# Two layers of attention and token mixer on one core: the mixer's first product in two passes instead of three, a third conversion buffer for VectorE's exponentials, loads tied to VectorE, and another order at the end of a layer

## The chip, the core and the metric

The kernel runs on one core of a Trainium2 chip. The core has TensorE (matrix products, into PSUM), VectorE, ScalarE and GpSimd, and a fifth engine, SyncE, that here only issues DMAs. The profile calls them PE, DVE, ACT, POOL and SP; PEld is TensorE's loading of weights. Each engine runs its own queue of instructions in order and waits for the others by semaphores. The metric is the device time of one launch in microseconds (us), as a median of several runs.

## The reference

The input is one sequence of 2048 tokens of width 640. Two blocks alternate, A, B, A, B, with the same weights both times.

```
def _A_ref(x, wqkv, wo):            # 32 heads of 20
    qkv = (x @ wqkv) ... q, k, v
    scores = einsum("bhqd,bhkd->bhqk", q, k) * 20 ** -0.5
    p = softmax(scores);  o = einsum("bhqk,bhkd->bhqd", p, v)
    return o @ wo
def _B_ref(x, w1, b1, w2, b2):      # mixes tokens: 2048 -> 1536 -> 2048
    u = gelu(einsum("bsd,sf->bdf", layernorm(x), w1) + b1)
    return transpose(einsum("bdf,fs->bds", u, w2) + b2)
x = x + A(layernorm(x));  x = x + B(layernorm(x))      # twice
```

The heads are narrow (20), so the two attention products are small and the 2 x 32 x 2048 x 2048 exponentials are the large part of the work.

## The kernel before

**Attention.** The queries are cut into four blocks of 512 (qb 0 to 3), the 32 heads into 8 groups of 4 (g), the keys into 16 tiles of 128 (kt). A unit is (qb, g, kt): four scores of 128 keys by 512 queries, one for each head of the group, which are called chunks here. There are 2048 chunks in a layer. The last block is cut into two halves of 256 queries, so that its first half is done early. For each chunk TensorE makes the scores S (`s_matmul`, L638), something takes the exponential, and TensorE adds P times V to the PSUM tile acc (`emit_PV`, L1253). V has a column of ones, which gives the softmax's denominators.

**Who takes the exponential.** ScalarE takes most: `emit_exp` (L708) works through tiles of three and of two chunks in turn (S to P). VectorE takes the rest, in pairs of chunks, by an approximation in integer and float steps: `ew` (L537) moves a chunk out of PSUM as an integer, `ey` (L597) shifts its fraction, `ey*ey` (L567) squares it, `et` (L571) and `Pd` (L580) finish the pair. The step L597 can be done by GpSimd or by VectorE: `ve_shift` hands it to GpSimd where VectorE is about to run a step that the planner counts as free of the memory port that the two engines share, and with a dependency on that moment (`after_vector`). What GpSimd hasn't got by then is done by VectorE in `shifted`. `ve_admit` decides when a chunk goes to VectorE. It refuses while VectorE's planned backlog is over VE_BACKLOG us, or while too many pairs wait in `ve_procs`, and it picks the unit whose chunk it takes by the backlog plus VE_MARGIN. The integers of a pair lie in the pool `vew` (2 buffers).

**The planner.** All of this is written out by a Python program that keeps a clock for each engine with planned durations, and lays the instructions into the queues in the order in which its clocks say they can run. ScalarE gets its tiles one after the other. In the time that TensorE has between them, `slot_work` (L1309) puts PV products, pieces of other products ("fills", `add_fill` and `fill_step`), or, if there is nothing, products with a zero matrix (`zeros`, L697), which keep TensorE busy and change nothing. The order of the DMAs on SyncE is not written out but left to the framework's own scheduler, which goes by the dependencies that it knows.

**The rest of a layer as fills.** When a query block is done, `enqueue_outproj` (L1031) adds the output product, "O" (L1044), and its sums with x become the rows x1; `do_ln2` (L865) normalises a tile of 128 rows into h2. The mixer's first product, "M" (`enqueue_mm1_partial`, L974, matmuls L992), sums over tokens, so that it can be begun with the rows that are there. It goes through 12 tiles of 128 columns of w1 (ft), each in two halves of 320 columns. M_GROUPS says which row tiles make one pass: 0 to 3, 4 to 7, and 8 to 13 (TAIL = 2 tiles are left for the end). The first two passes write their sums to a DRAM buffer, `uacc`: the half rows leave PSUM through VectorE to `ustg` (L1005) and go out by a DMA of GpSimd's queue, the second pass's with addition in the DMA (L1013). The last pass fetches the sums back (`fetch_row`, L958, a SyncE DMA into the places of buffers that are done with) and adds to them in SBUF (L1000). Each pass loads its piece of w1 for a column tile just ahead (`mm1_prefetch`, L970, two buffers `w1st`). The normalised rows of the first two passes lie in four buffers `h2st`; the later ones in the big buffer `hh`, which by then is free. The O products of blocks 0 and 1 have a gate: none starts while M products are left (`m_left`).

**The end of a layer** (`end_tiles`, L882). When ScalarE has done its last tile, the last PV and the normalisation of the last head group remain (L745 to L769, `attnT`). Fills that are left over are put in first. Then ScalarE loads the table for gelu (L884), TensorE writes zeros to two PSUM tiles (L697 on S), ScalarE copies the last two row tiles of x1 into them (L891), TensorE adds the last part of O (L895, in the order odd, then tile), VectorE and GpSimd take the statistics, ScalarE copies the sums back (L906), and ScalarE and VectorE normalise one tile each (L920, L923). `mixer_head` (L1666 on) then adds the last two row tiles of M, takes gelu, and starts the second product. After layer 0 that second product is fill work beside the next layer's attention; after layer 1 it runs alone to the end. The weights `w1l` that `mixer_head` needs are loaded over K's rows during the last units (`load_w1l`, L164).

Of the kernel before, what the change touches and what calls it, by code (L numbers as in the profile page):

```python
# [12 lines left out]
BF16 = mybir.dt.bfloat16  # L13
# [5 lines left out]
ACT = mybir.ActivationFunctionType  # L19
ALU = mybir.AluOpType  # L20
# [3 lines left out]
D = 640  # L24
# [10 lines left out]
    A0_LAG=2,  # L35
    VE_BACKLOG=4.0,
    VE_MARGIN=2.0,
    VE_LEAST=4,
# [39 lines left out]
def kernel(  # L78
# [12 lines left out]
    nc = tc.nc  # L91
# [3 lines left out]
    NT = S // 128  # L95
    NKT = NT
    NQB = S // 512
    NF = F // 128
# [35 lines left out]
    TAIL = 2  # L134
    M_GROUPS = [list(range(4 * p, 4 * p + 4)) for p in range(NQB - 2)] + [list(range(4 * (NQB - 2), NT - TAIL))]
    IN_HH = 4 * (NQB - 2)
    assert NF % 2 == 0
    uacc = [dpool.tile([F, D], F32, name=f"uacc{i}") for i in range(2)]
# [3 lines left out]
    mhalf = consts.tile([128, 1], F32, name="mhalf")  # L142
# [10 lines left out]
    x1lp = ctx.enter_context(tc.tile_pool(name="x1lp", bufs=1))  # L153
    x1last = x1lp.tile([128, 4, D], F32, name="x1last")
    hhp = ctx.enter_context(tc.tile_pool(name="hhp", bufs=1))
    hh = hhp.tile([128, NDT * S], BF16, name="hh")
# [7 lines left out]
    def load_w1l():  # L164
        for sti in range(TAIL):
            nc.sync.dma_start(out=w1l_view[:, sti, :], in_=B_w1[(NT - TAIL + sti) * 128:(NT - TAIL + sti + 1) * 128, :])

# [49 lines left out]
    def attention(st, x_in_ap, x_mid, uacc_l, feed, feed_stack):  # L217
# [16 lines left out]
        def open_late():  # L234
            def pool(name, bufs):
                late[name] = p1.enter_context(tc.tile_pool(name=f"{name}{layer}", bufs=bufs, reuse_waits="tile"))
            pool("xsp", 3 if x_in_ap.dtype == F32 else 2)
            pool("h2sp", 4)
            pool("w1sp", 2)
            pool("ustg", 2)  # L240
            pool("atp", NG + 4)
            pool("vew", 2)
            pool("vet", 1)
            pool("vey", 2)
            pool("vep", 3)
# [254 lines left out]
        def ve_admit(t):  # L500
# [297 lines left out]
        at_live = [0]  # L798
        m_left = [0]
        fill_queue = []  # L800
# [64 lines left out]
        def do_ln2(tt, x1s, end):  # L865
            def dst():
                if tt >= IN_HH:
                    assert check_hT_dead()
                    h2_tiles[tt] = h2_view[:, tt, :]
                else:  # L870
                    h2_tiles[tt] = late["h2sp"].tile([128, D], BF16, name="h2st")[:]
                return h2_tiles[tt]

            def after(e):
                ln_open.remove(tt)
                p = next(i for i, grp in enumerate(M_GROUPS) if tt in grp)
                if all(i in h2_tiles for i in M_GROUPS[p]):
                    enqueue_mm1_partial(p, e + DVE_TO_PE)
            ln_open.append(tt)
            ln_proc(x1s[:], True, dst, 3, end + DVE_NEXT, after)  # L880

        def end_tiles(sums):  # L882
            assert check_hT_dead() and TAIL == 2
            nc.scalar.activation(out=warm_act[:, 0:1], in_=mhalf[:, 0:1], func=ACT.Gelu_apprx_tanh, scale=1.0)  # L884
            gp = NG // 2 - 1
# [4 lines left out]
            for t, x1 in zip(sums, x1_end):  # L890
                nc.scalar.copy(out=t[:, 0:D], in_=x1)  # L891
            for odd in range(2):
                for ttl, t in enumerate(sums):
                    for c0, c1 in Y_CUTS:
                        pe(nc.tensor.matmul(t[:, c0:c1], lhsT=attnT[:, 256 * odd + ttl * 128:256 * odd + (ttl + 1) * 128],  # L895
                                            rhs=wo_pad[:, 2 * gp + odd, c0:c1], start=False, stop=(odd == 1),
                                            skip_group_check=True))
# [46 lines left out]
        def fetch_row(ft):  # L944
            if ft >= NF or ft in fetched:
                return
            if ft == len(st.ua):
# [8 lines left out]
                else:  # L956
                    return
            nc.sync.dma_start(out=st.ua[ft], in_=uacc_l[ft * 128:(ft + 1) * 128, :])  # L958
            fetched[ft] = pem["t"] + 5.0
# [6 lines left out]
        def mm1_prefetch(p, ft):  # L966
            if ft < NF and (p, ft) not in w1_of:
                group = M_GROUPS[p]
                w1st = w1_of[(p, ft)] = late["w1sp"].tile([128, len(M_GROUPS[-1]), 128], BF16, name="w1st")
                nc.sync.dma_start(out=w1st[:, 0:len(group), :],  # L970
                                  in_=B_w1[group[0] * 128:(group[-1] + 1) * 128, ft * 128:(ft + 1) * 128].rearrange(
                                      "(a s) f -> s a f", s=128))

        def enqueue_mm1_partial(p, ready):  # L974
# [3 lines left out]
            direct = p == len(M_GROUPS) - 1  # L978
            m_left[0] += 2 * NF
            rows = {}  # L980
# [3 lines left out]
            for ft in range(NF):  # L984
                for ci, (c0, c1) in enumerate(((0, D // 2), (D // 2, D))):
                    w = c1 - c0
                    mms = []
                    for sti in range(n_in):
                        def mm(t, sti=sti, ft=ft, c0=c0, c1=c1, w=w, ci=ci):
                            if sti == 0 and ci == 0:  # L990
                                mm1_prefetch(p, ft + 1)
                            pe(nc.tensor.matmul(t[:, 0:w], lhsT=w1_of[(p, ft)][:, sti, :],  # L992
                                                rhs=rows_in[sti][:, c0:c1], start=(sti == 0), stop=(sti == n_in - 1)))
                            m_left[0] -= sti == n_in - 1
                        mms.append(mm)

                    def evac(t, end, eng, ft=ft, c0=c0, c1=c1, w=w):
# [23 lines left out]
                    add_fill("M", 1e3 + p, mms, evac, w, ready=ready + (4.0 if p < NQB - 2 else 0.0), allow=later,  # L1021
                             gate=(lambda ft=ft: row_here(ft)) if direct else None)
# [8 lines left out]
        def enqueue_outproj(qb, ready):  # L1031
# [3 lines left out]
            for ttl in range(4):  # L1035
                tt = qb * 4 + ttl
                for ci, (c0, c1) in enumerate(((0, D // 2), (D // 2, D))):
# [12 lines left out]
                    def evac(t, end, eng, tt=tt, c0=c0, c1=c1, w=w, ci=ci):  # L1050
# [6 lines left out]
                        if ci == 1:  # L1057
                            nc.sync.dma_start(out=x_mid[tt * 128:(tt + 1) * 128, :], in_=x1s[:])
                            do_ln2(tt, x1s, end)
                            del tt_state[tt]  # L1060
                    add_fill("O", prio, mms, evac, w, ready=ready, gate=(lambda: m_left[0] == 0) if qb < NQB - 2 else None,
                             allow=lambda me, tt=tt: not any(o <= tt - 2 for o in ln_open))

        def enqueue_outproj_last(half, pairs, ready):
# [3 lines left out]
            if half == 0:  # L1068
                mm1_prefetch(NQB - 2, 0)
                for ft in range(4):  # L1070
                    fetch_row(ft)
            for ttl in range(2):
                tt = tt0 + ttl
                for ci, (c0, c1) in enumerate(((0, D // 2), (D // 2, D))):
# [13 lines left out]
                    def evac(t, end, eng, tt=tt, c0=c0, c1=c1, w=w, ci=ci):  # L1088
# [707 lines left out]
```

## Time and profile before

| | |
|---|---|
| time, median of 3 runs | 1780.67 us (1779.75 to 1782.98) |
| the profiled execution | 1779.18 us, of which 1777.4 us are the span shown |
| ScalarE busy | 1686.8 us (95%) |
| TensorE busy, with the zero products | 1686.2 us (95%) |
| VectorE busy | 1537.8 us (87%) |
| GpSimd busy | 339.3 us (19%) |
| ScalarE tiles of 3 / 2 / 1 chunks | 724 / 724 / 2 |
| chunks on VectorE (L537) | 474, in 237 pairs |
| steps L597 on GpSimd / on VectorE | 392 / 82, of 617 / 419 ns |
| half rows to ustg (L1005) | 96 of 481 ns |
| DMAs uacc<-ustg | 48, of which 24 with addition (894 ns of GpSimd each) |
| granted TensorE clock | full in every stretch |

The span has five stretches: a start of some 17 us, layer 0's attention to 831.5 us, the mixer's head and the start of layer 1's attention (from 869.5 us), that attention to 1707 us, and the last mixer to the end. Busy time of one engine is the union of its instructions; the mean duration of one can be longer than its share, because neighbours overlap: ScalarE's 1450 exponentials of 1377 ns mean take 1639.3 us together. A busy TensorE says little here, since the zero products count as busy.

### The profile page before, as it was taken

What the parts mean: (1) busy time and instruction counts of PE and PEld (TensorE: products, weight loads), DVE (VectorE), ACT (ScalarE), POOL (GpSimd) and SP (SyncE); (2) the same over time, 40 slices, a digit from 0 to 9 for tenths busy, and PEclk for the clock granted to TensorE, in tenths of its full rate; (3) what the DMA queues carried; (4) which work ended last, traced back from release to release, by engine and by line L of the source; (5) the groups of instructions that cost most, each with busy time, mean ns of one, the idle gap of its engine ahead of it and who ended that gap; (6) DMA issues with size and microseconds to landing.
All of it is one profiled execution on the core that took longest, in us unless ns stands there. A gap on an engine that the chain in (4) does not pass through costs nothing.

```text
span 1777.4 us, 42841 instructions
## 1 busy us (share of the span) xinstructions
PE 1686.2 (95%) x17848; PEld 668.0 (38%) x17929; DVE 1537.8 (87%) x2429; ACT 1686.8 (95%) x1518; POOL 339.3 (19%) x519
## 2 busy tenths in 40 slices
PE   8999999999999999999999999999999999999999
PEld 3333333333333344444444433233333333444445
DVE  7479999999999999998543469999999999999972
ACT  8999999999999999998779999999999999999970
POOL 2111111122233221121000001222222331212100
PEclk9999999999999999999999999999999999999999
DMA  4200000011117110123322100001112460101235
GB/s 121 27 1 1 1 1 2 20 38 64 53 53 124 28 58 13 31 57 91 110 81 79 52 11 2 1 2 38 54 42 75 83 114 24 61 3 48 63 113 179
DMA packets 106851, 89.71 MB, mean 50 GB/s; under 512 B 51744, under 2 KB 88224, under 8 KB 106656
## 3 DMA queue, kind: packets, MB, share of 16 engines
q1 hardware_dynamic: 97664, 71.22, 13.7%
q0 software_dynamic: 8992, 15.75, 4.6%
q8 instruction: 140, 2.29, 0.6%
q14 instruction: 55, 0.45, 0.1%
HBM read 55.48 MB, written 31.46 MB: 49 GB/s over the span
## 4 chain that ended last, share of the span: by engine, by line
ACT 51%; issue 23%; PE 19%; DVE 3%; DMA 2%; SPq 0%; POOL 0%; another core or an unknown queue 0%; ACTq 0%; POOLq 0%; DVEq 0%
ACT P L708 51%; PE S L638 5%; PE acc L1253 2%; PE ya L1679 2%; PE misc L992 2%; PE acc L697 1%; PE misc L1104 1%; DMA uacc<-ustg 1%; PE um L1666 1%; DMA w1st<-in_B_w_dram 1%; DVE ew L537 1%; PE ya L1688 1%; DVE et L571 1%; PE yb L1679 1%; PE misc L1598 0%
## 5 line engine op out<-in xcount | busy, mean ns | idle before, releaser
L708 ACT ACTIVATE P<-S 128x1024 bf16<-128x1024 f32 (+1 forms) x1450 | 1639.3, 1377 | 15.5 <-PE S L638 15.2
L638 PE MATMUL S<-QTq,KT 32*128 32x512 bf16 (+1 forms) x4519 | 584.5, 337 | 70.1 <-ACT P L708 54.3
L597 POOL TENSOR_SCALAR ey<-ew 128x512 f16<-128x512 uint16 x392 | 242.0, 617 | 1039.5 <-DVE et L571 384.7
L638 PEld LDWEIGHTS <-KT 32*128 32x128 bf16 x5137 | 232.4, 91 | 531.8 <-issue 506.3
L1253 PE MATMUL acc<-P,Vaug 128*32 128x512 bf16 (+1 forms) x4502 | 366.0, 343 | 0.0
L537 DVE TENSOR_SCALAR ew<-Dt 128x512 int32<-128x512 f32 x474 | 323.6, 683 | 18.2 <-PE Dt L638 9.4
L697 PE MATMUL acc<-zr,zw 128*32 128x512 bf16 x4292 | 336.1, 384 | 1.3 <-POOL zr L151 1.2
L580 DVE SCALAR_TENSOR_TENSOR Pd<-ew,et 128x1024 int16<-128x1024 int16 x237 | 296.5, 1251 | 1.1
L571 DVE SCALAR_TENSOR_TENSOR et<-ey,ew 128x1024 f32<-128x1024 f16 x237 | 290.1, 1224 | 2.0
L638 PE MATMUL Dt<-QTq,KT 32*128 32x512 bf16 (+1 forms) x618 | 182.2, 332 | 0.0
L1253 PEld LDWEIGHTS <-Vaug 128*32 128x32 bf16 x5120 | 102.9, 94 | 177.7 <-issue 168.3
L567 DVE TENSOR_TENSOR ey<-ey 128x1024 f16<-128x1024 f16 x237 | 162.0, 684 | 5.0 <-POOL ey L597 0.9
L697 PEld LDWEIGHTS <-zw 128*32 128x32 bf16 x4504 | 113.6, 96 | 103.7 <-issue 60.7
L838 POOL TENSOR_TENSOR rstd<-veps,mhalf 128x1 f32<-128x1 f32 x60 | 50.5, 842 | 250.9 <-DVE veps L836 204.6
L1253 PE MATMUL acc<-Pd,Vaug 128*32 128x512 bf16 (+1 forms) x618 | 93.2, 334 | 0.0
L1104 PE MATMUL misc<-hh,wq_pad 128*128 128x512 bf16 x276 | 83.4, 383 | 2.2 <-issue 1.6
L992 PE MATMUL misc<-h2st,w1st 128*128 128x320 bf16 x384 | 74.6, 303 | 3.2 <-DMA w1st<-in_B_w_dram 2.5
L992 PEld LDWEIGHTS <-w1st 128*128 128x128 bf16 x672 | 52.3, 97 | 62.2 <-issue 45.7
L745 DVE STREAM_TRANSPOSE T<-acc 128x512 f32<-128x512 f32 (+1 forms) x81 | 56.3, 695 | 19.4 <-PE acc L1253 19.3
L1044 PE MATMUL misc<-wo_pad,attnT 128*128 128x320 bf16 x384 | 72.6, 302 | 0.2
L1104 PE MATMUL misc<-hh,wk_pad 128*128 128x512 bf16 x211 | 65.0, 383 | 2.5 <-issue 2.1
L357 DVE CAST KT<-misc 128x512 bf16<-128x512 f32 x48 | 32.9, 685 | 20.1 <-PE misc L1104 19.9
(144 smaller groups left out, 1161.0 us busy)
## 6 DMA issues: line engine op xcount, KB each, us to landing
uacc<-ustg POOLq DMA_DIRECT2D x48, 320.0 KB, 4.2
w2s<-in_B_w_dram SPq DMA_DIRECT2D x16, 768.0 KB
x1in<-xd SPq DMA_DIRECT2D x24, 320.0 KB
w1st<-in_B_w_dram SPq DMA_DIRECT2D x48, 128.0 KB
xd<-x2s SPq DMA_DIRECT2D x16, 320.0 KB
xin<-xd SPq DMA_DIRECT2D x16, 320.0 KB
w1st<-in_B_w_dram SPq DMA_DIRECT2D x24, 192.0 KB
xd<-x1s SPq DMA_DIRECT2D x12, 320.0 KB
```

The lines of the kernel that those rows point to most:

```text
L537: nc.vector.tensor_scalar(out=w[:, slot, :], in0=Dt[:, :], scalar1=127.0 * FIX, scalar2=0.0, op0=ALU.add, op1=ALU.max)
L567: nc.vector.tensor_tensor(out=y, in0=y, in1=y, op=ALU.mult)
L571: nc.vector.scalar_tensor_tensor(out=box["t"][:, 0:512 * k], in0=ve_y.pop(p)[:, 0:512 * k], scalar=MANT_C * MANT_K ** 2, in1=frac, op0=ALU ...
L580: nc.vector.scalar_tensor_tensor(out=bits, in0=whole, scalar=128.0, in1=box["t"][:, 0:512 * k], op0=ALU.mult, op1=ALU.add)
L597: return engine.tensor_scalar(out=out_ap, in0=in_ap, scalar1=MANT_K / FIX, scalar2=-MANT_K * MANT_S, op0=ALU.mult, op1=ALU.add)
L638: pe(nc.tensor.matmul(out_ap[:, c0:c0 + w], lhsT=KT[32 * j:32 * j + 32, g, kt * 128:(kt + 1) * 128], rhs=get_QT(st, qb)[32 * j:32 * j + 32 ...
L697: pe(nc.tensor.matmul(bank[32 * j:32 * j + 32, 0:w], lhsT=zw[:], rhs=zr[:, :, 0:64].to_broadcast([128, w // 64, 64]), start=start, stop=st ...
L708: nc.scalar.activation(out=P[:, 0:ncs, :].rearrange("p a b -> p (a b)"), in_=St[:, 0:ncs, :].rearrange("p a b -> p (a b)"), func=ACT.Exp, ...
L992: pe(nc.tensor.matmul(t[:, 0:w], lhsT=w1_of[(p, ft)][:, sti, :], rhs=rows_in[sti][:, c0:c1], start=(sti == 0), stop=(sti == n_in - 1)))
L1044: pe(nc.tensor.matmul(t[:, 0:w], lhsT=attnT[g][:, ttl * 128:(ttl + 1) * 128], rhs=wo_pad[:, g, c0:c1], start=(g == 0), stop=(g == NG - 1)))
L1104: pe(nc.tensor.matmul(t[:, :], lhsT=wpad[:, dt_, g, :], rhs=hT[:, dt_, tb * 512:(tb + 1) * 512], start=(dt_ == 0), stop=(dt_ == NDT - 1)))
L1253: pe(nc.tensor.matmul(acc[32 * j:32 * j + 32, a0:a0 + w], lhsT=Vaug[:, (kt * H + hh_) * VW:(kt * H + hh_) * VW + 32], rhs=P[:, slot, c0:c0 ...
```

## The change

It has six parts.

1. M goes in two passes: rows 0 to 7, then rows 8 to 13. The first pass writes its sums to `uacc` once, with no addition; `w1st` holds 8 blocks instead of 6; the normalised rows 0 to 7 lie in the buffer `x1last` (which is used for the last rows only later), and the pool `h2sp` goes. The gate on the O products of blocks 0 and 1 goes; instead those of the last block wait until the first pass is through (`low_left`).
2. `vew` has three buffers, and `ve_admit` lets two pairs wait ahead of the one that is worked on.
3. VE_BACKLOG is 7 instead of 4 us, VE_MARGIN 3 instead of 2 us.
4. `fetch_row` and `load_w1l` are tied to the VectorE instruction that stands before them in the program.
5. In `end_tiles` the two copies come ahead of the load of the gelu table.
6. There, the last part of O is made tile by tile.

```diff
-    VE_BACKLOG=4.0,
-    VE_MARGIN=2.0,
+    VE_BACKLOG=7.0,
+    VE_MARGIN=3.0,
...
-    M_GROUPS = [list(range(4 * p, 4 * p + 4)) for p in range(NQB - 2)] + [list(range(4 * (NQB - 2), NT - TAIL))]
     IN_HH = 4 * (NQB - 2)
+    M_GROUPS = [list(range(IN_HH)), list(range(IN_HH, NT - TAIL))]
...
+    h2_low = x1last[:].rearrange("p a d -> p (a d)").bitcast(BF16).rearrange("p (t d) -> p t d", t=8)
...
-            nc.sync.dma_start(out=w1l_view[:, sti, :], in_=B_w1[(NT - TAIL + sti) * 128:(NT - TAIL + sti + 1) * 128, :])
+            after_vector(nc.sync.dma_start(out=w1l_view[:, sti, :],
+                                           in_=B_w1[(NT - TAIL + sti) * 128:(NT - TAIL + sti + 1) * 128, :]))
...
-            pool("h2sp", 4)
...
-            pool("vew", 2)
+            pool("vew", 3)
...
-                if len(ve_procs) > 1:
+                if len(ve_procs) > 2:
...
-                    h2_tiles[tt] = late["h2sp"].tile([128, D], BF16, name="h2st")[:]
+                    h2_tiles[tt] = h2_low[:, tt, :]
...
-            nc.scalar.activation(out=warm_act[:, 0:1], in_=mhalf[:, 0:1], func=ACT.Gelu_apprx_tanh, scale=1.0)
...
             for t, x1 in zip(sums, x1_end):
                 nc.scalar.copy(out=t[:, 0:D], in_=x1)
-            for odd in range(2):
-                for ttl, t in enumerate(sums):
+            nc.scalar.activation(out=warm_act[:, 0:1], in_=mhalf[:, 0:1], func=ACT.Gelu_apprx_tanh, scale=1.0)
+            for ttl, t in enumerate(sums):
+                for odd in range(2):
...
-            nc.sync.dma_start(out=st.ua[ft], in_=uacc_l[ft * 128:(ft + 1) * 128, :])
+            after_vector(nc.sync.dma_start(out=st.ua[ft], in_=uacc_l[ft * 128:(ft + 1) * 128, :]))
...
-                w1st = w1_of[(p, ft)] = late["w1sp"].tile([128, len(M_GROUPS[-1]), 128], BF16, name="w1st")
+                w1st = w1_of[(p, ft)] = late["w1sp"].tile([128, max(map(len, M_GROUPS)), 128], BF16, name="w1st")
...
-                        if p == 0:
-                            nc.gpsimd.dma_start(out=dst, in_=stg[:])
-                        else:
-                            nc.gpsimd.dma_start(out=dst, in_=stg[:], accum_op=ALU.add)
+                        nc.gpsimd.dma_start(out=dst, in_=stg[:])
...
-                    add_fill("O", prio, mms, evac, w, ready=ready, gate=(lambda: m_left[0] == 0) if qb < NQB - 2 else None,
+                    add_fill("O", prio, mms, evac, w, ready=ready,
...
-                    add_fill("O", 500.0, mms, evac, w, ready=ready)
+                    add_fill("O", 500.0, mms, evac, w, ready=ready, gate=lambda: low_left[0] == 0)
```

Because the planner works the whole order out anew, the instruction streams differ in many places. Counted in the two programs (before to after): ScalarE tiles of three chunks 724 to 719, of two 724 to 719, of one 2 to 3; chunks on VectorE 474 to 498; steps L597 on VectorE 82 to 2, on GpSimd 392 to 496; half rows to ustg 96 to 48; DMAs uacc<-ustg 48 to 24; loads of w1st 48 of four blocks and 24 of six to 24 of eight and 24 of six; zero products up by 132 matmuls, that is 33 of four. The streams are the same up to about 117 us, and again from the mixer's head of layer 0 to where VectorE takes its first chunks of layer 1.

More of the change, by code (lines that the diff above doesn't have):

```diff
@@ L154 @@
     x1last = x1lp.tile([128, 4, D], F32, name="x1last")
+    assert IN_HH <= 8
+    h2_low = x1last[:].rearrange("p a d -> p (a d)").bitcast(BF16).rearrange("p (t d) -> p t d", t=8)
     hhp = ctx.enter_context(tc.tile_pool(name="hhp", bufs=1))
@@ L798, in attention @@
         at_live = [0]
-        m_left = [0]
+        low_left = [2 * NF]
         fill_queue = []
@@ L870, in dst @@
                 else:
-                    h2_tiles[tt] = late["h2sp"].tile([128, D], BF16, name="h2st")[:]
+                    assert len(vready) == 2 * NT
+                    h2_tiles[tt] = h2_low[:, tt, :]
                 return h2_tiles[tt]
@@ L978, in enqueue_mm1_partial @@
             direct = p == len(M_GROUPS) - 1
-            m_left[0] += 2 * NF
             rows = {}
@@ L993, in mm @@
                                                 rhs=rows_in[sti][:, c0:c1], start=(sti == 0), stop=(sti == n_in - 1)))
-                            m_left[0] -= sti == n_in - 1
+                            low_left[0] -= not direct and sti == n_in - 1
                         mms.append(mm)
@@ L1020, in later @@
                         return True
-                    add_fill("M", 1e3 + p, mms, evac, w, ready=ready + (4.0 if p < NQB - 2 else 0.0), allow=later,
+                    add_fill("M", 1e3 + p, mms, evac, w, ready=ready + (0.0 if direct else 4.0), allow=later,
                              gate=(lambda ft=ft: row_here(ft)) if direct else None)
@@ L1068, in enqueue_outproj_last @@
             if half == 0:
-                mm1_prefetch(NQB - 2, 0)
+                mm1_prefetch(1, 0)
                 for ft in range(4):
```

## The prediction

> **What bounds the kernel now.** The page comes first, then ScalarE's groups, its stretches, its timeline, the chain, and last the end of a layer.
>
> ```profile
> PE 1686.2 (95%) x17848; PEld 668.0 (38%) x17929; DVE 1537.8 (87%) x2429; ACT 1686.8 (95%) x1518; POOL 339.3 (19%) x519
> ...
> ACT 51%; issue 23%; PE 19%; DVE 3%; DMA 2%; SPq 0%; POOL 0%; another core or an unknown queue 0%; ACTq 0%; POOLq 0%; DVEq 0%
> ```
>
> TensorE's 95% is padded with zero products, so it proves nothing; the chain names ScalarE. Its groups by form and the busy time by stretch (columns: stretch, length, then TensorE, weight load, VectorE, ScalarE, GpSimd, clock, DMA) say how hard:
>
> ```profile
> L708 ACT ACTIVATE P<-S 128x1536 bf16<-128x1536 f32 x724 | 1150.0, 1588 | 5.5 <-PE S L638 5.3
> L708 ACT ACTIVATE P<-S 128x1024 bf16<-128x1024 f32 x724 | 845.6, 1168 | 10.0 <-PE S L638 10.0
> ...
> 45.00:445.00 400.00, 379.01 (x3515) 132.18 (x3541) 359.01 (x533) 399.99 (x355) 70.70 (x107) 1.00 0.07 17
> 540.00:640.00 100.00, 94.51 (x1090) 33.35 (x1089) 96.23 (x132) 98.84 (x89) 28.29 (x42) 1.00 0.38 71
> 1250.00:1350.00 100.00, 93.47 (x821) 32.48 (x823) 98.20 (x144) 100.00 (x90) 25.56 (x42) 1.00 0.16 51
> ```
>
> In attention ScalarE has no gap: 399.99 us of 400. So a microsecond of exponentials taken off it is a microsecond of time, as long as the others keep up; VectorE, at 96 to 98%, is the next. Outside the start of each layer ScalarE waits at two places, 561 and 1432 us:
>
> ```profile
> 561.65 1.02 ACT L708 ACTIVATE P<-S 128x1024 bf16<-128x1024 f32 x1 [0.57 <-PE S L638]
> 563.18 37.79 ACT L708 ACTIVATE P<-S 128x1536 bf16<-128x1536 f32 x33 [0.51 <-PE S L638]
> 1432.13 8.23 ACT L708 ACTIVATE P<-S 128x1536 bf16<-128x1536 f32 x7 [0.63 <-PE S L638]
> ```
>
> The chain from 536 us says why (columns: start, length):
>
> ```profile
> 548.48 5.28 DMA uacc<-ustg
> ...
> 553.77 0.34 SPq L958
> ...
> 554.21 6.38 DMA w1st<-in_B_w_dram
> ...
> 560.64 0.58 PE misc L992 x3
> ```
>
> A fetch of M's sums (L958) stands in SyncE's queue ahead of a load of w1, waits for the sum to be written, and TensorE stops for the weights. The end of layer 0, from the timeline:
>
> ```profile
> 831.51 1.28 ACT L884 ACT_TABLE_LOAD   x1
> 832.13 0.72 PE L992 MATMUL misc<-hh,w1st 128*128 128x320 bf16 x4
> 832.78 1.05 PE L697 MATMUL S<-zr,zw 128*32 128x512 bf16 x16
> 833.49 1.32 ACT L891 COPY S<-x1last 128x640 f32<-128x640 f32 x2 [0.49 <-ACT warm_act L884]
> 833.72 0.45 DVE L1000 TENSOR_TENSOR KT<-misc,KT 128x320 f32<-128x320 f32 x1
> 834.24 0.43 PE L895 MATMUL S<-wo_pad,attnT 128*128 128x512 bf16 x2 [0.41 <-ACT S L891]
> 835.67 0.90 DVE L905 BATCH_NORM_STATS2 bnst<-S 128x6 f32<-128x320 f32 x2 [1.50 <-PE S L895]
> ```
>
> The copies wait for the zeros (0.71 us after their start), not for the table, which is in at 833.0.
>
> **The change, part by part.** Counts are those of the two programs.
>
> *ScalarE, -10.9 us.* It loses 5 tiles of three chunks and 5 of two and gets one of one. The records overlap: 1996.9 us of single durations fill 1639.3 us, 0.247 us for each of 1450. So a tile costs 1.341, 0.921 or 0.407 us, and 5 x 1.341 + 5 x 0.921 - 0.407 = 10.9. All of it lies where ScalarE is full.
>
> *VectorE, about +1 us, at nothing.* 24 chunks more cost 24 x 0.683 (L537) + 12 x (0.684 + 1.224 + 1.251) = 54.3 us. The shorter M saves 48 x 0.481 (L1005) = 23.1, and 80 shifts that go to GpSimd save 80 x 0.419 = 33.5. Sum -2.3. But the 72 of 474 records of L571 and L580 that had a GpSimd shift beside them took 1.37 us against 1.21 without: 72 x 0.16 = 11.5 us over 392 shifts, 0.03 each, or 3.1 us for 104 more. The extremes are 0 and a whole shift each, 104 x 0.617 = 64 us; I take 3.1, since it is these same instructions. VectorE was idle 16.6 us from 445 to 835 us and 12.4 from 1250 to 1700, so +0.8 is covered; without that cover late pairs are next.
>
> The Trainium skill has a rule against this part (SBUF — State Buffer, Who interferes with whom): a VectorE instruction with two SBUF inputs contends with a GpSimd instruction that reads SBUF, and the loser blocks for the whole instruction. The trace agrees that they hinder each other, but with 0.16 us where they met. By the rule in full the sum would be that of rival B below.
>
> *Pairs that come late, +1.0 us.* This is what a larger backlog risks. I counted, in ScalarE time, how far the last step of a pair stands in the program ahead of the first PV that reads it. Before, 6 of 237 stand within 2.3 us; after, 31 of 249. In the trace those six were done 0.05 to 0.81 us ahead of their use; the one at 0.05 was just waited for. One in six of 31 is 5 waits, at 0.2 us each, an estimate from the two smallest slacks, 0.05 and 0.24 us. Ends: 0, and 31 x 0.617 = 19 us. TensorE works in order, so behind a late pair stand the next scores, and ScalarE waits for them.
>
> *SyncE's queue, -1.7 us.* With the sums written once and the fetches tied to VectorE, the fetches stand behind the w1 loads of their pass, and the sums are long written: the waits of 0.57 + 0.51 + 0.63 us go. What the ties add: each fetch waits for a VectorE step (1.25 us at most), and behind it stand w1st and xin loads. The last pass issues its w1st loads some 4.5 us apart (1668.94, 1673.45, 1677.97) and their packets land within 2.3, which covers it. Ends: -1.7 and 0. A first-pass load now has 1024 packets; 512 took 1.9 us and 768 took 2.25, so some 2.6, against 16 matmuls of 0.135 = 2.2 us if nothing stood between. With scores and PV between, a column tile of half as many took 4.5 us. At nothing.
>
> *GpSimd and zeros, at nothing.* +104 x 0.617 - 24 x 0.894 = +43 us on an engine that is 19% busy. 33 more zero products of 0.22 us (16 matmuls in 1.05) fill slots that would be empty. The new gate opens near the program's instruction 12,900, and the products behind it come from 17,900 on. Normalising into x1last instead of h2st is the same step (0.60 to 0.65 us).
>
> *The end of layer 0, +2.4 us.* After the last PV now stand 23 M matmuls, not 4. Eleven (0.135 each) run from 832.13 to 833.6, while VectorE normalises; the next twelve need the first half row out of its bank, which VectorE does after the normalisation, as at 833.72 to 834.17. So 834.2 + 12 x 0.135 = 835.85 for the zeros instead of 832.78, +3.07, and copies and L895 move with them. Tile by tile the first tile needs no second copy: its statistics start 0.81 us after 834.24, not after 834.86, -0.62. The table load (1.28 + 0.20) now runs in ScalarE's idle time of 1.87 us before L906. The second load of w2 waits for the last of these matmuls, near 836 instead of 828.5; it is first used at 853.5 and takes 5.2 us; the loads of x1in and wv queued behind it are used from 853 and 865 on.
>
> *The end of layer 1, +0.5 us.* Twelve M matmuls are new: zeros from 1707.09 to 1708.71, copy 0.71 later, L895 0.75 after that, statistics 0.81 after that, 1710.98 against 1710.52. Ends for both layers: 0, if normalisation hides it, and +5.
>
> Sum: -10.9 - 1.7 + 1.0 + 2.9 = -8.7 us. The profiled execution took 1779.18 us, 1.5 below the median of the runs: 1770.5 on its base, **1772.0 us** on the median's. No change that is under 0.2% (3.6 us) can be told from none.
>
> **The rivals.**
>
> *A': the ends and the late pairs cost nothing.* 1780.67 - 12.6 = 1768.1 us. For it: normalisation runs beside the extra matmuls. Against: the second twelve wait for VectorE.
>
> *B, slower: pairs come late because GpSimd's shifts block VectorE.* Place: the 31 close pairs. If one whole shift delays each, 31 x 0.617 = 19.1 instead of 1.0: 1790.1 us. It makes the kernel slower from 0.43 us a pair on ((12.2 + 1.0)/31). For it: two slacks under 0.25 us. Against: where they met it was 0.16 us, and the shifts are laid beside steps that took 683 ns with and without one.
>
> *C, no gain: the larger w1 loads stop TensorE.* 22 loads, each 2.6 - 2.2 = 0.44 us late, 9.7 us: 1781.7 us. Against: the 4.5 us above.
>
> That the change doesn't do what it says is out: the program has the counts.
>
> **How the numbers follow.** The forecast has 0.70 (its own range 1768.5 to 1777: all ends but those of B and C), A' 0.11, C 0.08, B 0.11. From 1767 (A' with the 0.9 us by which the lowest run lies under the median) to 1778 lies 0.81. Faster are the forecast and A' but for its edge, 0.79; same C and that edge, 0.10; slower B, 0.11.
>
> **What would show it.** ScalarE's L708 near 1628.4 us (1639.3 - 10.9) with under 16 us of idle before it; no wait of 0.5 us near 561 and 1432; L580 near 1.25 us; the end from ScalarE's last exponential to the first um matmul 2.4 us longer in layer 0 and 0.5 in layer 1. I am wrong if ScalarE waits often for S while TensorE waits for Pd (B) or w1st (C), or if VectorE's busy time rises by tens of us.

## The result and the profile after

The changed kernel takes 1770.67 us (median of 4 runs, 1770.4 to 1772.69); the kernel before took 1780.21 us on the same chip (4 runs, 1779.38 to 1782.98). The ratio is 0.995, with a 95% interval of 0.9938 to 0.9962. The forecast was 1772.0 us in a range from 1767 to 1778, so 1.3 us too much.

The page of the changed kernel, its engines, then ScalarE's exponentials by form (busy time of the group, mean of one | idle time before them):

```profile
PE 1683.8 (95%) x17978; PEld 671.5 (38%) x18058; DVE 1538.4 (87%) x2361; ACT 1676.4 (95%) x1509; POOL 386.6 (22%) x599
...
L710 ACT ACTIVATE P<-S 128x1536 bf16<-128x1536 f32 x719 | 1135.6, 1579 | 6.2 <-PE S L640 5.9 <-PE acc L1252 0.2
L710 ACT ACTIVATE P<-S 128x1024 bf16<-128x1024 f32 x719 | 833.9, 1160 | 9.4 <-PE S L640 9.4
```

L710 is L708 of before; its 1441 tiles together are busy for 1629.0 us. VectorE is as busy as before, GpSimd 47 us more. The stretches, in the same columns as for before:

```profile
45.00:445.00 400.00, 379.04 (x3655) 131.16 (x3680) 358.25 (x511) 399.86 (x354) 87.98 (x132) 1.00 0.05 11
540.00:640.00 100.00, 95.65 (x1055) 35.81 (x1053) 97.13 (x131) 100.00 (x90) 28.77 (x47) 1.00 0.15 45
```

ScalarE still has no gap in attention, also not between 540 and 640 us, where it had lost 1.16 us. Inside layer 0 its timeline has one idle entry of 0.16 us; near 1432 us there is none. The one new wait stands at the start of layer 1:

```profile
902.44 2.03 ACT L710 ACTIVATE P<-S 128x1536 bf16<-128x1536 f32 x2 [0.23 <-PE S L640]
906.60 7.38 ACT L710 ACTIVATE P<-S 128x1536 bf16<-128x1536 f32 x7 [2.12 <-PE S L640]
```

Before, the second of these was 1.35 us and the first was absent, so this is 1.0 us lost. The windows of 1 us there show why; the third figure from the end is the granted clock:

```profile
901.00:902.00 1.00, 1.00 (x6) 0.26 (x4) 0.25 (x1) 1.00 (x2) 0.00 (x0) 0.50 0.00 0
904.00:905.00 1.00, 0.95 (x5) 0.41 (x5) 0.49 (x1) 0.48 (x1) 0.00 (x0) 1.00 0.00 0
```

TensorE had half its clock from 900.4 to 903.8 us; this is called the dip below. The kernel before had full clock there in its profile.

The end of layer 0, from the timeline (start, duration, group, idle time before it and what ended it); ScalarE's last exponential ends at 825.52:

```profile
825.96 0.85 PE L994 MATMUL misc<-hh,w1st 128*128 128x320 bf16 x5
826.65 0.98 PE L994 MATMUL Dt<-hh,w1st 128*128 128x320 bf16 x6
...
828.05 0.98 PE L994 MATMUL misc<-hh,w1st 128*128 128x320 bf16 x6 [0.42 <-DVE KT L1002]
828.87 0.98 PE L994 MATMUL S<-hh,w1st 128*128 128x320 bf16 x6
...
830.43 1.05 PE L699 MATMUL S<-zr,zw 128*32 128x512 bf16 x16 [0.58 <-DVE KT L1002]
...
831.88 1.33 PE L898 MATMUL S<-wo_pad,attnT 128*128 128x512 bf16 x7 [0.41 <-ACT S L893]
...
832.69 0.90 DVE L908 BATCH_NORM_STATS2 bnst<-S 128x6 f32<-128x320 f32 x2 [2.32 <-PE S L898]
```

The 23 products of M stand ahead of the zeros, and twice TensorE waits for VectorE to empty a bank (L1002). The zeros start 4.91 us after the last exponential; before, it was 1.29 (832.78 against 831.49).

The whole span, cut where ScalarE's exponentials begin and end (us):

| piece | before | after | change | forecast |
|---|---|---|---|---|
| start to the first exponential | 16.91 | 17.72 | +0.81 | 0 |
| exponentials of layer 0 | 814.58 | 807.80 | -6.78 | -11.6 for both layers |
| to the first of layer 1 | 37.99 | 40.98 | +2.99 | +2.4 |
| exponentials of layer 1 | 837.45 | 833.23 | -4.22 | (above) |
| to the end | 70.47 | 71.17 | +0.70 | +0.5 |
| span | 1777.4 | 1770.9 | -6.5 | -8.7 |

The profiled execution of after was 2.0 us above its median, that of before 1.0 below. The experiments tell what of this belongs to the change.

### The profile page after: what moved, and what is told of

The parts are those of the page before. It is cut to its first block, busy times and chain, and to the rows that moved or that the text cites. A ratio compares the mean times of both kernels' runs of the same rounds, so it can differ in the third digit from the quotient of the medians.

```text
span 1770.9 us, 42935 instructions
## 1 busy us (share of the span) xinstructions
PE 1683.8 (95%) x17978; PEld 671.5 (38%) x18058; DVE 1538.4 (87%) x2361; ACT 1676.4 (95%) x1509; POOL 386.6 (22%) x599
## 5 line engine op out<-in xcount | busy, mean ns | idle before, releaser
L710 ACT ACTIVATE P<-S 128x1536 bf16<-128x1536 f32 (+2 forms) x1441 | 1629.0, 1368 | 15.6 <-PE S L640 15.3
L599 POOL TENSOR_SCALAR ey<-ew 128x512 f16<-128x512 uint16 x496 | 306.7, 618 | 1017.2 <-DVE et L573 387.3
L1252 PE MATMUL acc<-P,Vaug 128*32 128x512 bf16 (+1 forms) x4470 | 361.5, 344 | 0.8 <-ACT P L710 0.3
L539 DVE TENSOR_SCALAR ew<-Dt 128x512 int32<-128x512 f32 x498 | 339.4, 681 | 18.7 <-PE Dt L640 12.4
L699 PE MATMUL acc<-zr,zw 128*32 128x512 bf16 x4436 | 344.0, 383 | 1.4 <-POOL zr L151 1.2
L582 DVE SCALAR_TENSOR_TENSOR Pd<-ew,et 128x1024 int16<-128x1024 int16 x249 | 310.7, 1248 | 1.5
L573 DVE SCALAR_TENSOR_TENSOR et<-ey,ew 128x1024 f32<-128x1024 f16 x249 | 303.5, 1219 | 2.0
L640 PE MATMUL Dt<-QTq,KT 32*128 32x512 bf16 (+1 forms) x650 | 191.5, 332 | 0.0
L569 DVE TENSOR_TENSOR ey<-ey 128x1024 f16<-128x1024 f16 x249 | 172.6, 693 | 0.5
L994 PE MATMUL misc<-x1last,w1st 128*128 128x320 bf16 x384 | 71.6, 302 | 0.0
```

The source lines that it names most:

```text
L539: nc.vector.tensor_scalar(out=w[:, slot, :], in0=Dt[:, :], scalar1=127.0 * FIX, scalar2=0.0, op0=ALU.add, op1=ALU.max)
L569: nc.vector.tensor_tensor(out=y, in0=y, in1=y, op=ALU.mult)
L573: nc.vector.scalar_tensor_tensor(out=box["t"][:, 0:512 * k], in0=ve_y.pop(p)[:, 0:512 * k], scalar=MANT_C * MANT_K ** 2, in1=frac, op0=ALU ...
L582: nc.vector.scalar_tensor_tensor(out=bits, in0=whole, scalar=128.0, in1=box["t"][:, 0:512 * k], op0=ALU.mult, op1=ALU.add)
L599: return engine.tensor_scalar(out=out_ap, in0=in_ap, scalar1=MANT_K / FIX, scalar2=-MANT_K * MANT_S, op0=ALU.mult, op1=ALU.add)
L640: pe(nc.tensor.matmul(out_ap[:, c0:c0 + w], lhsT=KT[32 * j:32 * j + 32, g, kt * 128:(kt + 1) * 128], rhs=get_QT(st, qb)[32 * j:32 * j + 32 ...
```

## The experiments

My theory was that ScalarE is the bound, so that the gain is the exponentials taken off it plus SyncE's waits, less the longer ends. Against it stood: that the shorter M carries the gain, that the settings alone do, that late pairs or the shared port cost much, and that the ends cost nothing.

**The changed kernel once more** (no edit).

> The changed kernel once more, unchanged, beside the others. Its first profile had a span 6.5 us shorter than the profile before, while the medians lie 9.5 us apart. If that profile's late start (first exponential at 17.72 us instead of 16.91) and its granted clock of 0.999 were accidents of one execution, this profile's span is near 1769 us and the ratio to the kernel before again 0.994 to 0.996. If they belong to the change, the span is again near 1771 us.

Measured: 1771.38 us, ratio 0.9953 (0.9939 to 0.9966). The first exponential starts at 17.21 us, so 0.5 of the 0.81 us was that execution's. The half clock is there again, from 899.9 to 903.3 us, and the span is 1770.5 us. Neither expectation held whole: the start moves between executions, the dip came back. But such a dip belongs to single executions. 3.41 us at half clock lower the mean granted clock of an execution to 0.999, and of the nine executions of the changed kernel four have 0.999 (1771.38 to 1772.69 us; both profiled ones are among them) and five have 1.000 (1770.40 to 1770.81). The kernel before, beside this run, had less than 1.000 in 8 of 21 executions. Three kernels below that have the same exponentials run that stretch at full clock in their profiles, and their layer 1 takes 832.0 us, not 833.2. With them (the kernel without ties: start 16.81, layers 807.81 and 832.01, ends 40.98 and 71.19) the change is -0.1 - 6.77 + 2.99 - 5.44 + 0.72 = -8.6 us.

**Without the VectorE part.**

```diff
-    VE_BACKLOG=7.0,
-    VE_MARGIN=3.0,
+    VE_BACKLOG=4.0,
+    VE_MARGIN=2.0,
...
-            pool("vew", 3)
+            pool("vew", 2)
...
-                if len(ve_procs) > 2:
+                if len(ve_procs) > 1:
```

> The change without its VectorE part: two buffers of converted pairs, at most two chains, backlog 4 and margin 2 as before; M in two passes, the pinned loads and the new last chain stay. My theory (the exponentials taken off ScalarE carry the gain): the program has 723 tiles of three, 722 of two and 3 of one chunk, so ScalarE loses 1.341 + 2 x 0.921 - 0.407 = 2.8 us; SyncE's waits -1.7; the ends, with 21 and 9 products of M behind the last PV where the changed kernel has 23 and 12 and measured +2.99 and +0.72, some +3.2. Sum -1.3: 1778.9 us, ratio 0.999. Rival (the shorter M, which takes 48 copies off VectorE and 24 summing writes off the queues, carries the gain): at least half of the 9.5 us, ratio 0.997 or less.

Measured: 1778.49 us, ratio 0.9994 (0.9985 to 1.0003). The two layers' exponentials took 811.52 and 836.31 us, 4.2 less than before, the ends 40.89 and 70.86, 3.3 more. My theory's -1.3 lies in the interval, the rival's 0.997 does not. The shorter M by itself frees VectorE, but with the old settings and two buffers the planner gives it only three pairs more.

**The settings alone, on the kernel before.** (The third buffer can't be tried there: the room for it comes from the pool `h2sp`, which goes with the third pass.)

```diff
-    VE_BACKLOG=4.0,
-    VE_MARGIN=2.0,
+    VE_BACKLOG=7.0,
+    VE_MARGIN=3.0,
```

> The kernel before with backlog 7 and margin 3 and nothing else: M in three passes, two buffers of converted pairs. It has 723, 722 and 3 tiles, so ScalarE loses 2.8 us; GpSimd takes 80 shifts more, as in the changed kernel; 25 and 13 products of M stand behind the last PVs, with the old order of the last chain: ends +3 + 0.6 and +0.8 + 0.6, some +5. My theory: -2.8 + 5 = +2, 1781.5 us, ratio 1.001; the settings are worth nothing without the third buffer. Rival (the settings are what brings the gain): ratio 0.997 or less.

Measured: 1790.8 us, ratio 1.0053 (1.0035 to 1.0071): worse than both theories. The chain from 561 us (start, length):

```profile
561.66 5.04 DMA uacc<-ustg
...
566.72 0.34 SPq L958
...
567.15 5.12 DMA w1st<-in_B_w_dram
572.27 0.05 issue
572.32 0.72 PE misc L992 x4
```

It is the chain of the kernel before: a fetch waits for a sum, the load of w1 stands behind it, and TensorE for the load. Here ScalarE then loses 0.88 and 0.90 us, and the clock is at 0.79 between 575 and 580. The five pieces are +0.45, +1.13, +5.11, +0.68 and +2.73 us: the waits eat the 2.8 us of exponentials, and both ends are longer, with 25 and 13 products of M behind the last PVs. (This execution also has half clock from 17.3 to 20.7 us, where ScalarE loses 1.15 us.) So in this run the three passes don't bear the closer packing; that the two passes do is what they are worth.

**The settings and the two passes, but two buffers.**

```diff
-            pool("vew", 3)
+            pool("vew", 2)
...
-                if len(ve_procs) > 2:
+                if len(ve_procs) > 1:
```

> The change with backlog 7 and margin 3, but two buffers of converted pairs and at most two chains. The program has 721, 720 and 3 tiles: ScalarE loses 3 x 1.341 + 4 x 0.921 - 0.407 = 7.3 us. Waits -1.7; 13 and 27 products of M stand behind the last PVs, ends some +3.5. My theory: -5.5, 1774.7 us, ratio 0.997: the third buffer is worth the rest, 3 to 4 us. Rival (the settings alone give all of it, the third buffer nothing): ratio 0.995, as the change.

Measured: 1778.61 us, ratio 0.9997 (0.9988 to 1.0006), 4 us above my theory. The exponentials took 811.04 and 834.63 us, 6.4 less than before where the counts and the waits said 9.0; the ends 39.51 and 74.96, 6.0 more where I said 3.5. The end of layer 1 is the larger miss: 27 products of M stand there, and TensorE waits 1.5 us for VectorE between them. The settings give nothing measurable without the third buffer. The other way round, the third buffer with the old settings, was not run, so what the settings add to the buffer is open.

**The ends in another order.** The zeros and the copies come first, half of M's rest ahead of L898 (the line has moved to L900), half behind it and ahead of the last normalising step. Of the zero products that follow fewer are left. `open_tiles` holds the zeros and the copies that stood in `end_tiles`; `one_fill` does one half row of a column tile of M.

```diff
-        while fs["cur"] is not None or fill_queue:
-            fill_step(tail_alloc)
-        end_tiles(sums)
+        open_tiles(sums)
+        for _ in range((len(fill_queue) + (fs["cur"] is not None)) // 2):
+            one_fill()
+        held = end_tiles(sums, one_fill)
...
             spread(1)
+            held = 0
+            while (n := one_fill()):
+                held += n
```

> The change with another order of the last work of a layer: the zeros and the two copies into them stand directly behind the last PV, and of the column tiles of M that are left half stand ahead of the last output projection (L898) and half behind it, in the place of some of the zero products there. My theory (the end of a layer costs because the zeros, copies and L898 stand behind these products): L898 starts 3.3 us earlier in layer 0 and 1.3 in layer 1, so 4.6 us less than the changed kernel: 1766.1 us, ratio 0.992. Rival (the end is set by the loads behind it, w2 and x1in, or by VectorE, which has the same work): nothing, ratio 0.995.

Measured: 1765.67 us, ratio 0.9921 (0.9909 to 0.9934); the changed kernel beside it had 0.9953. The end of layer 0 from its timeline:

```profile
825.12 1.05 PE L699 MATMUL S<-zr,zw 128*32 128x512 bf16 x16
...
825.82 1.32 ACT L890 COPY S<-x1last 128x640 f32<-128x640 f32 x2 [1.03 <-issue]
...
827.60 1.25 PE L900 MATMUL S<-wo_pad,attnT 128*128 128x512 bf16 x7
...
828.42 0.90 DVE L910 BATCH_NORM_STATS2 bnst<-S 128x6 f32<-128x320 f32 x2
...
828.69 0.98 PE L1000 MATMUL misc<-hh,w1st 128*128 128x320 bf16 x6
```

The copies now run while M and the normalisation do, and the statistics start 3.63 us after the last exponential (824.79), not 7.17. The gaps between the layers are 37.44 us instead of 40.98 and the last piece 69.73 instead of 71.17: 5.0 us less, where I had said 4.6. It is the fastest kernel here, 13.6 us under the kernel before.

**The same ends with two buffers.** The edit is the two before together.

> The reordered ends of the run before (zeros and copies first, half of M's rest behind L898) with two buffers of converted pairs and at most two chains. With two buffers and the old ends the two spans of exponentials were 811.04 and 834.63 us, 5.9 us more than the 807.81 and 832.04 with three buffers, and the ends 39.51 and 74.96, 8.3 us above those of the reordered kernel. My theory (the ends are a matter of M's rest behind the last PV, the exponentials one of the buffers): the ends become as short as with three buffers, so the third buffer alone is worth 5.9 us: 1771.6 us, ratio 0.9954. Rival (two buffers also lengthen the ends): 1773 to 1778 us, ratio 0.996 to 0.999.

Measured: 1774.14 us, ratio 0.9967 (0.9956 to 0.9978). The rival holds: the exponentials are as with the old ends (811.01 and 834.28 us), the gap between the layers is short (36.51), but the last piece is 75.51 us. TensorE's waits name it (us, times, longest):

```profile
PE Dt L1000 <- DMA w1st<-in_B_w_dram: 3.0, 1, 3.0
```

The last piece of w1 is issued at 1701.75, after the last exponential, since M lags there with two buffers. Right behind this wait the clock is at half from 1708.1 to 1711.5 us, and the profiled execution is 2.1 us above its median, so a part of the 75.51 us is that execution's. Between this run and the one with three buffers, the third buffer is worth 0.0046 of the time, 8 us by the medians; of it 5.4 us are exponentials (3.2 and 2.2); the rest is put down to this lag, which no run tests alone.

**More work on the shared port.** GpSimd does one more shift on constant data after each first shift of a pair.

```diff
+            if len(ve_shifted[p]) == 1:
+                shift(nc.gpsimd, late["y"][:], late["in"])
             ve_shifted[p].append(slot)
```

> The changed kernel, in which GpSimd does one more shift (a copy of L599 on constant data, into a tile that nobody reads) after each first shift of a pair: 248 more, 153 us of GpSimd, beside VectorE's steps; the order of everything else is the same. The forecast's price: in the changed kernel the 179 records of L569, L573 and L582 that had a shift beside them were longer by 46 x 0.043 + 47 x 0.111 + 86 x 0.112 = 16.8 us over 496 shifts, 0.034 us each, so 248 more are 8 us of VectorE, at most 248 x 0.16 = 40 us where each meets one of them; with VectorE at 97% in attention the time grows by 0 to 15 us, ratio to before 0.995 to 1.004. Rival B (the loser blocks for the whole shift): 248 x 0.617 = 153 us on VectorE, of which its idle time in attention covers some 30: over 100 us slower, ratio 1.05 or more, and L573 and L582 above 1.4 us in the mean.

Measured: 1790.78 us, ratio 1.0061 (1.0047 to 1.0075), some 19 us slower than the changed kernel. VectorE's three steps on two SBUF inputs, by form (busy, mean ns), and then GpSimd's extra shift:

```profile
L585 DVE SCALAR_TENSOR_TENSOR Pd<-ew,et 128x1024 int16<-128x1024 int16 x249 | 319.7, 1284 | 1.5
L576 DVE SCALAR_TENSOR_TENSOR et<-ey,ew 128x1024 f32<-128x1024 f16 x249 | 319.3, 1282 | 2.0
L572 DVE TENSOR_TENSOR ey<-ey 128x1024 f16<-128x1024 f16 x249 | 190.8, 766 | 0.5
```

```profile
L602 POOL TENSOR_SCALAR spare<-wo_pad 128x512 f16<-128x512 uint16 x247 | 252.6, 1023 | 19.6
```

In the changed kernel the three VectorE steps took 310.7, 303.5 and 172.6 us; they grew by 9.0 + 15.8 + 18.2 = 43.0 us, 0.17 for each extra shift. Not 0.034 us as forecast, and not the 0.617 of rival B. The extra shift itself takes 1.02 us in the mean, not 0.62. What makes up these means stands in the single records; three in a row from the timeline:

```profile
302.20 1.25 DVE L576 SCALAR_TENSOR_TENSOR et<-ey,ew 128x1024 f32<-128x1024 f16 x1
302.46 1.47 POOL L602 TENSOR_SCALAR spare<-wo_pad 128x512 f16<-128x512 uint16 x1
303.48 1.51 DVE L585 SCALAR_TENSOR_TENSOR Pd<-ew,et 128x1024 int16<-128x1024 int16 x1
```

The shift begins during the first step and ends 0.48 us after it; the next step begins during the shift and ends 1.06 us after that. So it is throughout. In all 153 meetings of over 0.15 us that the step began, the shift ended 0.47 to 0.48 us behind the step. Of the 330 that the shift began, in 321 the step ended a fixed time behind the shift: 1.06 to 1.08 us, for L572 0.53 to 0.54; in the other nine both began within 0.05 us and the shift was the one to wait. So whichever comes second waits for the end of the first, and loses what is left of it: anything from nothing to a whole instruction. VectorE's busy time rose by 35 us, and some half of that reached the end.

**Pairs closer to their use.**

```diff
-    VE_MARGIN=3.0,
+    VE_MARGIN=0.0,
```

> The changed kernel with a margin of 0 instead of 3: ScalarE has the same 719, 719 and 3 tiles and VectorE the same 249 pairs, but 108 pairs, not 31, stand within 2.3 us of ScalarE time of their first use, 37 within 1.4, not 6. Products of M behind the last PVs: 14 and 24. My price of late pairs (one close pair in six is waited for, 0.2 us each): 3.6 us instead of 1.0, so 2.6 slower than the changed kernel, ratio to before 0.9965. Rival A' (close pairs cost nothing): as the changed kernel, 0.995. Rival B's price (0.617 each): 47 us slower, ratio 1.02.

Measured: 1779.4 us, ratio 1.0002 (0.9993 to 1.0011): no gain is left, with the same tiles on ScalarE. TensorE's waits, in us, times and the longest:

```profile
PE acc L1252 <- DVE Pd L582: 6.2, 7, 1.4
```

Seven times a pair is waited for, 0.9 us each. What one costs, from the timeline, and then the window of 1 us behind it:

```profile
1070.92 1.22 DVE L582 SCALAR_TENSOR_TENSOR Pd<-ew,et 128x1024 int16<-128x1024 int16 x1
...
1072.19 0.39 PE L1252 MATMUL acc<-Pd,Vaug 128*32 128x512 bf16 x2 [1.44 <-DVE Pd L582]
...
1073.15 1.90 PE L699 MATMUL acc<-zr,zw 128*32 128x512 bf16 x16
...
1076.54 1.45 ACT L710 ACTIVATE P<-S 128x1536 bf16<-128x1536 f32 x1 [1.21 <-PE Dt L640]
```

```profile
1074.00:1075.00 1.00, 1.00 (x16) 0.45 (x12) 1.00 (x1) 1.00 (x2) 0.00 (x0) 0.50 0.00 0
```

TensorE stands for 1.44 us, and then its clock is at half from 1072.9 to 1076.3 us: 16 zero products take 1.90 us instead of 1.05, and the scores come late. ScalarE loses 0.39 us to the stand (at 1072.96) and 1.21 behind the zero products, and 0.89 and 0.88 us more around a second stand, at 1078.9 and 1083.0. Against 807.81 and 832.01 us without ties, the exponentials of the two layers take 0.8 and 6.4 us more; the last piece takes 2.3 us more and the one between the layers 0.7 less. The two end pieces go the way of M's rest (24 and 14 products behind the last PVs, not 12 and 23), so some 7 of the 8.8 us are the late pairs and the half clock, which in this execution came a third time, from 1697.6 to 1701.0. My price of a late pair was far too low, rival B's too high.

**Without the ties.**

```diff
-            after_vector(nc.sync.dma_start(out=st.ua[ft], in_=uacc_l[ft * 128:(ft + 1) * 128, :]))
+            nc.sync.dma_start(out=st.ua[ft], in_=uacc_l[ft * 128:(ft + 1) * 128, :])
```

and the same for the loads of `w1l`.

> The changed kernel without the two ties of loads to VectorE (fetches of M's sums L961 and the loads of w1's last rows). In SyncE's queue four fetches of each layer then stand between the w1 loads of the first pass, each waiting for a sum that is just being written; with the ties all fetches stand behind that pass. ScalarE and VectorE have the same program. My theory (the waits of 0.5 to 0.6 us near 561 and 1432 us of the kernel before came from this order): one to four such waits a layer come back, 1 to 5 us, ratio to before 0.9955 to 0.998. Rival (writing the sums once is enough; the ties do nothing): 0.995.

Measured: 1770.6 us, ratio 0.9949 (0.9936 to 0.9961); no wait near 561 or 1432 us. The rival holds, but not because the fetches need not wait. In layer 0 four of them stand between the w1 loads, and each is issued 0.02 to 0.06 us after a sum has landed. SyncE's waits for sums are nearly those of the kernel before (in us, times, longest), there and then here:

```profile
SPq L958 <- DMA uacc<-ustg: 31.9, 8, 5.7
```

```profile
SPq L960 <- DMA uacc<-ustg: 30.0, 8, 4.6
...
533.56 0.34 SPq L960 DMA_DIRECT2D hh<-uacc  x1
536.59 0.37 SPq L972 DMA_DIRECT2D w1st<-in_B_w_dram  x1
```

What has changed is the load behind the fetch. In the kernel before it followed 0.1 us behind (554.11 to 554.21), so it had been waiting; here it comes 2.3 to 3.7 us later, so the fetch holds up nothing. Two things differ: the loads of the first pass are 6.8 to 7.7 us apart, where those of the second pass before came 4.5 to 4.9 apart up to the first wait, and these four sums land 2.5 to 3.8 us after their issue, where those with addition took 4.5 to 6.6. Which of the two does more isn't shown. The two passes are what removes the waits; the ties bring nothing here.

**The last chain in the old order.**

```diff
-            for ttl, t in enumerate(sums):
-                for odd in range(2):
+            for odd in range(2):
+                for ttl, t in enumerate(sums):
```

with the table load ahead of the copies.

> The changed kernel with the last chain as before: the table is loaded ahead of the two copies into the sums, and L898 goes by halves over both tiles instead of tile by tile. My theory: the first tile's statistics wait for the second copy again, 0.62 us in each layer, and the table load is hidden since the copies wait for the zeros: 1.2 us slower than the changed kernel, ratio to before 0.9957. Rival (the copies cover it): nothing, 0.995.

Measured: 1772.0 us, ratio 0.9956 (0.9942 to 0.9969); the medians are too close to decide. The pieces decide: 41.60 against 40.98 us between the layers and 71.80 against 71.19 at the end, 0.62 and 0.61, as in my theory. The place of the table load went back in the same run, so that it costs nothing is not shown apart.

## Why the prediction was right, step by step

*ScalarE, -10.9 us: right.* 1639.3 became 1629.0 us of busy time, -10.3; the forecast was 1628.4. The pitch of 1.341, 0.921 and 0.407 us a tile was measured where ScalarE has no gap, so it carried over. That such a microsecond is one of time is borne out by the layers: -12.2 us without the dip of the clock, of which 1.7 are the waits.

*VectorE, +0.8 us, covered: right.* 1537.8 became 1538.4 us, Pd 1.248 us in the mean where 1.25 was said. But the price of 0.03 us a shift is a property of where the planner lays the shifts, not of the port: shifts laid elsewhere cost 0.17 us each. Had the change put its 104 shifts beside the steps that share the port, they would have cost some 18 us of VectorE (104 x 0.174, an estimate). The Trainium skill (SBUF — State Buffer, Who interferes with whom) has the two engines share an exclusive lock; the single records of that run agree, with their fixed 0.48 and 1.07 us behind the end of the first. The prediction, and rival B with it, took the rule to mean a whole shift lost for each shift; what is lost is the rest of a shift, and only where the two meet: 16.8 us over the 496 shifts of the changed kernel. The rule was also right in which instructions meet: the move out of PSUM (L539, L542 in the run with more shifts) took 676 ns there with a shift beside it and 674 without.

*Late pairs, +1.0 us: too much here, and mis-priced.* In the trace of after, four pairs were done only 0.05 us ahead of their use, where before it was one; that is as close as any comes. The one wait of TensorE for a pair over 0.15 us was 0.2 us. Margin 0 shows that a pair which is really late costs far more than the 0.2 us: 0.9 us of TensorE, and then the clock. The range of that step should have had a steep upper end that begins close by; 31 close pairs cost next to nothing, and 108 took most of the gain.

*SyncE's queue, -1.7 us: right in amount, wrong in cause.* All three waits went. Not because the fetches stand behind the loads, as the step had it: without the ties they stand between them and wait for their sums, but the loads behind them then have 2.3 us and more to spare.

*The end of layer 0, +2.4 us: mis-sized, +2.99.* The -0.62 of the tile-by-tile order is confirmed. The zeros came not 3.07 but 3.62 us later: TensorE waits for L1002 twice, 0.42 us ahead of the second twelve products and 0.58 ahead of the zeros, whose bank the last product had used; I had counted only the first. *The end of layer 1, +0.5: +0.72.*

*Costed at nothing:* the larger w1 loads (rival C) stayed hidden; the waits of TensorE's weight loads for w1st fell from 4.6 us to 0.3. The start (+0.81 and +0.30 us in two executions, -0.1 in the kernel without ties) moves by itself. The half clock at 900 us, 1.2 us in the profiled executions, was in neither the sum nor a rival.

So the forecast of -8.7 us stands against -8.6 in the pieces without the dip. That it is so close is in part luck: the layers came out 0.6 us better than forecast (-12.2 against -11.6), mostly because late pairs cost so little, and the ends 0.8 worse (3.7 against 2.9). Rival A' was right on the pairs and wrong on the ends; B and C did not come to pass.

What stays open: why the clock halves near 900 us in the two profiled executions of the changed kernel and not in those of three others with the same exponentials. The traces show that all changes of the granted clock in one execution lie whole multiples of 3.413 us apart (in the changed kernel 894.29, 3.41 and 866.99 us, that is 262, 1 and 254 times), and that this grid lies elsewhere in each execution: a step of it begins 30.4 and 30.5 us after layer 1's first exponential in the two profiles with the dip, and 30.1, 31.2 and 31.6 in the three without. That the place of the grid decides would fit, but isn't shown.

## What to carry to other kernels

When one engine is full, count what is taken off it at its pitch in the full stretch; but look at the two ends of the stretch as well, where work that was "fill" becomes the path: moving the last fills behind the step that others wait for gained another 5 us. A planner's margin against late operands can be worth more than the wait it avoids, because a stalled TensorE may then run at half clock for 3.4 us. And parts of a change that give nothing alone (0.9994 for the two passes, 1.0053 for the settings, 0.9997 for both) can still make a gain together (0.9953): judge them by leaving one out as well as by putting one in. A mean, too, can hide its two cases: 0.17 us a shift was a wait for the rest of an instruction where two met, and nothing elsewhere.

## What the runs showed of the hardware

- TensorE's granted clock fell to one half for 3.4 us after a stand of 1.4 us (1072.9 to 1076.3 us at margin 0), and products of the same shape took nearly twice as long: 1.90 us for sixteen instead of 1.05. The Trainium skill (TensorE: Matmul & The Clock Gate, Part 1) has half the clock after an idle window of some 3.4 us; here the 3.4 us before were not idle: by the windows of 1 us from 1069 on, TensorE was busy for 1.00, 0.75, 0.00 and 0.81 us. A stand does not always do it: with two buffers TensorE stood for 1.51 us before 1704.17 us, and its clock stayed full to the end of the span.
- Each of the nine stretches at half clock inside the profiled spans lasted 3.41 us, and in every profile the changes of the clock lie on a grid of that length.
- A GpSimd shift and a VectorE step on two SBUF inputs do not run side by side: the one that comes second waits for the end of the first. The shift, 0.62 us alone, then ended 0.47 to 0.48 us behind the step; the steps, 1.21 us alone (L572 0.67), ended 1.06 to 1.08 us (0.53 to 0.54) behind the shift. In the mean, with a shift beside it, L572 took 854 instead of 672 ns, L576 1367 instead of 1209 and L585 1338 instead of 1207.
